# A hand-ordered linear-attention and FFN kernel: a neighbouring order of its 1639 steps

## The chip, the cores and the metric

The kernel runs on one core of a Trainium2 chip. The metric is device time in microseconds (us) of one execution, the median of several runs. Engines: TensorE (PE; its weight loads are shown apart as PEld), VectorE (DVE), ScalarE (ACT), GpSimd (POOL) and SyncE (SP), which only issues DMAs here. Each engine runs its own instructions strictly in the order in which the program lists them.

## The reference

```python
# q, k, v, alpha: (4, 8, 768, 48)
for t in range(S):                                    # 768 steps, a 48x48 state per head
    state = alpha[:, :, t, :, None] * state + einsum('bhd,bhe->bhde', k[:, :, t], v[:, :, t])
    y[:, :, t] = einsum('bhd,bhde->bhe', q[:, :, t], state)
x = y.transpose(0, 2, 1, 3).reshape(3072, 384)
h = x @ w_in                                          # w_in 384 x 2048
g = where(h > 0, h, exp(min(h, 0)) - 1)
out = g @ w_out                                       # w_out 2048 x 384
```

A gated linear attention with a decay per channel feeds a feed-forward network (FFN) with an ELU between its two products.

## The kernel before, in words

Time is cut into 24 windows of 128 steps (6 for each of 4 batches; eight heads as four pairs). The FFN works on 9 blocks of tokens: three narrow ones of 256, six wide ones of 384, and on 8 (narrow: pairs of) or 16 slices `j` of the hidden dimension. FFN products are split into a high and a low fp32r part, three matmuls for one product.

The program is a list of tokens, `ORDER`, written out by hand: `NAME.i` is one step for window, slice or block `i`, and a second number is a half, a part or a slice. The tokens are issued in exactly this order. Other tables give the PSUM bank (`BANKS`) and the SBUF slot (`SLOTS`) of each tile in order of use, and which engine takes a step: windows in `KAV`, `KBV`, `SQV` and slices in `WLV` run `KA`, `KB`, `SQ` and `WL` on DVE, the others on POOL; pairs in `GQ` have `GL` on POOL, the others on DVE.

The steps that matter here, by window `i`:

- Loads, all issued by SP: `LA` (alpha), `LB` (k for half 0, q for half 1), `L` (all of a window), `LV` (v), `F` (a slice of weights, as int64 words).
- DVE `SC` (L299): running product P of alpha. ACT `LN` (L311), `EX` (L317): R = 1/P. `KA` (L325), `KB` (L330), DVE `KC` (L335): the scaled keys; `KC` reads R. `SQ` (L353, L356): scaled queries. ACT `PC` (L340): a check sum of P, written over R.
- PE `TP` (L378): transposes the keys, ACT `KN` (L408) copies them out of PSUM; for later windows DVE `T` (L388) does it.
- PE `U` (L490, L472): two state products u[0] and u[1] of a window. For windows 0 and 1 they lie in one PSUM bank, in different columns; for later ones in two banks, which they share with the scores of `S`.
- `UA` reads u[0] (L507 on ACT for windows 0, 1, 6, 12, 18; L509 on DVE else); DVE `UB`, `UC` (L509, L538, L540) read u[1] and write the state for the next window. PE `UP` (L516) adds the state.
- PE `S` (L443, L427): scores, DVE `MK` (L460, L455) masks them out of PSUM. PE `YL` (L551), ACT `Y3` (L593), PE `Y` (L605, L551, L556): the output of a window; ACT `XH` (L619, L620), PE `XP` (L624) and `XL` (L642, L646): its high and low part, the input of the FFN.
- Weights: ACT `KW` (L686), DVE `DA` (L702), `DB` (L707) decode a slice, ACT `WH` (L734) and `WL` (L754) split it.
- FFN for block b, slice j: PE `A.b.j` (L786) is the first product, ACT `RA` (L795), `RB` (L800), DVE `RC` (L806) the ELU, ACT `GH` (L812) and `GL` (L819) split it, PE `O.b.j` (L835) is the second product. `Z` (L845) writes a block out.
- PE `X` (L208): filler matmuls with no result, in the first 12 us only.

Lines that a sentence can't say as well:

```python
def bank(name):
    return psa.tile([128, 512], F32, name=name, tag=f"pa{next(banks)}")
...
u = bank("u")[:, 0:2 * NP * D].rearrange("p (x n e) -> p x n e", x=2, n=NP)
d["u"] = [u[:, 0], u[:, 1]]
...
def PC(i):
    nc.scalar.activation(out=win[i]["R"], in_=pw(i), func=AF.Copy, accum_out=chk_p[:, 1, i:i + 1])
```

Of the kernel before, what the change touches and what calls it, by code (L numbers as in the profile page):

```python
# [63 lines left out]
WH.4 WL.4 KW.1.0 DA.1.0 RB.0.0 RC.0.0 DB.1.0 SC.5 RA.0.1 GH.0.0 UB.3 GL.0.0 L.4 RB.0.1 Y3.3 F.8 WH.1 A.0.3 RA.0.3 WL.1
WH.3 WL.3 XP.2 XL.2 F.10 RB.0.3 RC.0.1 Y.3 XH.3 LV.7 RC.0.3 UC.3 XL.3 KW.3 A.0.2 DA.3 SC.4 LN.5 A.1.1 DB.3 RA.0.2 RB.0.2
RA.1.1 EX.5 KA.5 O.0.0 RB.1.1 A.1.0 KW.4 RC.0.2 RC.1.1 RA.1.0 RB.1.0 GH.0.1 GL.0.1 GH.0.2 LN.4 F.12 DA.4 DB.4 WH.10
RC.1.0 GH.1.0 LC.1 A.1.3 KB.5 GL.1.0 WH.7 WH.8 WL.7 GH.1.1 F.9 GL.0.2 GL.1.1 A.1.2 O.0.1 RA.1.2 RB.1.2 WL.10 EX.4 O.1.0
CA.1 RC.1.2 KA.4 WH.5 WL.8 O.1.1 GH.1.2 WL.5 RA.1.3 RB.1.3 GL.1.2 A.1.5 RC.1.3 GH.0.3 F.14 ZV.6 KW.6 DA.6 CB.1 F.11
A.0.4 O.1.2 RA.0.4 RB.0.4 A.0.5 RA.1.5 O.0.2 KB.4 DB.6 WH.14 GL.0.3 SQ.4 KC.4 S.4 WH.12 RB.1.5 RA.0.5 RC.0.4 L.6 KC.5
RC.1.5 DA.5 GH.0.4 KW.5 LV.6 MK.4 TP.4 RB.0.5 GH.1.5 RC.0.5 KN.4 TP.5 KN.5 LC.3 DB.5 GH.1.3 O.0.3 PC.4 SQ.5 CA.3 LV.5  # L70
U.5 WH.9 WL.12 S.5 MK.5.1 MK.5.0 A.0.6 WH.11 WL.11 RA.0.6 GL.1.3 O.1.3 LV.4 U.4 RB.0.6 RC.0.6 PC.5 CB.3 SC.6 WL.9 LN.6
EX.6 GL.0.4 A.1.4 RA.1.4 RB.1.4 UA.4 UB.4 UC.4 L.7 SC.7 LN.7 KA.6 LC.2 RC.1.4 WL.14 A.1.6 KB.6 A.1.7 UA.5 GH.0.5 O.0.4
EX.7 KA.7 KB.7 RA.1.7 KC.6 RA.1.6 RB.1.7 RC.1.7 F.13 GH.1.4 GH.0.6 Y.5 RB.1.6 KC.7 T.7.2 GL.1.5 XH.5 Y.4 PC.7 RC.1.6
# [78 lines left out]
47251074320475130677466246740246271537464206
"""
# [942 lines left out]
```

## Time and profile before

| | us |
|---|---|
| median of 3 runs | 463.92 |
| lowest and highest run | 463.62, 464.58 |
| the profiled execution's own time | 463.38 |
| its span, first to last instruction | 461.6 |
| PE busy | 454.2 |
| DVE, ACT, POOL busy | 349.8, 327.7, 214.2 |

The span is 1.78 us shorter than that execution's time, and that execution is 0.54 us below the median of the runs. The rows further down are of this execution. A row of a timeline begins with its start and its length; brackets give the idle time of the engine before it and what ended that.

### The profile page before, as it was taken

To read this page: it belongs to the slowest core of one execution; us is meant where nothing else is said; L and a number is where in the kernel's file an instruction comes from. 1 tells how busy PE (TensorE), PEld (TensorE's weight loads), DVE (VectorE), ACT (ScalarE), POOL (GpSimd) and SP (SyncE) were. 2 spreads that over 40 slices of the span, in tenths; PEclk is the share of its full clock that TensorE was granted. 3 is DMA by queue.
4 is the path that set the end of the run, shared out by engine and by line. 5 is a ranking of instruction groups with operands and counts; after the bars stand their busy time and mean duration, and the time that the engine had idled before them with its cause. 6 is when DMAs were issued, how large, how long until landed. Compare 5 with 4: busy or idle time off the path is not lost.

```text
span 461.6 us, 12451 instructions
## 1 busy us (share of the span) xinstructions
PE 454.2 (98%) x4942; PEld 439.5 (95%) x4942; DVE 349.8 (76%) x756; ACT 327.7 (71%) x741; POOL 214.2 (46%) x185
## 2 busy tenths in 40 slices
...
GB/s 249 416 411 318 286 104 158 156 154 104 104 233 0 189 102 175 133 47 134 46 177 139 126 58 189 153 73 155 78 121 35 121 45 53 28 42 85 36 4 58
DMA packets 23859, 61.10 MB, mean 132 GB/s; under 512 B 3184, under 2 KB 10864, under 8 KB 23792
## 3 DMA queue, kind: packets, MB, share of 16 engines
...
q8 instruction: 41, 0.67, 0.6%
...
## 4 chain that ended last, share of the span: by engine, by line
PE 89%; DVE 4%; ACT 3%; DMA 3%; issue 1%; SPq 0%; DVEq 0%
PE h L786 39%; PE o L835 38%; PE y L556 4%; PE q L472 2%; PE q L427 2%; DMA vs<-in_vv_dram 2%; PE y L551 1%; ACT w L734 1%; DVE raw L702 1%; DVE wm L707 1%; DMA qka<-in_qka_dram 1%; ACT gh L812 1%; PE y L605 1%; ACT r L800 1%; PE sc L443 0%
## 5 line engine op out<-in xcount | busy, mean ns | idle before, releaser
L786 PE MATMUL h<-xt,w 128*128 128x384 f32 (+1 forms) x1296 | 200.0, 310 | 0.3 <-DVE r L806 0.3
L786 PEld LDWEIGHTS h<-xt,w 128*128 128x128 f32 x1296 | 190.7, 190 | 1.5 <-DVE r L806 0.4
L835 PE MATMUL o<-w,gh 128*128 128x384 f32 x768 | 188.3, 327 | 0.0
L819 POOL TENSOR_TENSOR gl<-r,gh 128x384 fp32r<-128x384 f32 (+1 forms) x90 | 106.4, 1189 | 158.1 <-ACT gh L812 101.8
L835 PEld LDWEIGHTS o<-w,gh 128*128 128x128 f32 x768 | 134.1, 189 | 0.5
L835 PE MATMUL o<-w,gl 128*128 128x384 f32 x384 | 125.3, 326 | 0.0
L795 ACT ACTIVATE r<-h 128x384 f32<-128x384 f32 (+1 forms) x120 | 60.3, 509 | 55.2 <-PE h L786 49.1
L388 DVE STREAM_TRANSPOSE kn<-qka 32x128 f32<-32x128 f32 x256 | 77.4, 303 | 4.2
L806 DVE SCALAR_TENSOR_TENSOR r<-r,h 128x384 f32<-128x384 f32 (+1 forms) x90 | 51.1, 577 | 37.9 <-ACT r L800 31.9
L835 PEld LDWEIGHTS o<-w,gl 128*128 128x128 f32 x384 | 72.6, 189 | 0.2 <-POOL gl L819 0.2
L800 ACT ACTIVATE r<-r 128x384 f32<-128x384 f32 (+1 forms) x120 | 64.0, 543 | 2.0
L812 ACT CAST gh<-r 128x384 fp32r<-128x384 f32 (+1 forms) x90 | 46.4, 529 | 18.6 <-DVE r L806 16.1
L356 POOL TENSOR_TENSOR st<-qka,P 64x512 f32<-64x512 f32 x34 | 43.0, 1263 | 17.4 <-DVE P L299 16.1
L455 DVE TENSOR_TENSOR st<-q,mask 64x256 f32<-64x256 f32 x76 | 32.1, 422 | 9.2 <-PE q L427 6.0
L325 POOL TENSOR_TENSOR qka<-qka,R 128x512 f32<-128x512 f32 x16 | 21.0, 1313 | 29.9 <-ACT R L317 24.7
L806 DVE SCALAR_TENSOR_TENSOR h<-r,h 128x384 f32<-128x384 f32 (+1 forms) x30 | 17.4, 588 | 20.7 <-ACT r L800 20.3
L299 DVE TENSOR_TENSOR_SCAN P<-qka,first 128x516 f32<-128x516 f32 (+1 forms) x25 | 30.7, 1233 | 0.5 <-DMA qka<-in_qka_dram 0.3
L819 DVE TENSOR_TENSOR gl<-h,gh 128x384 fp32r<-128x384 f32 (+1 forms) x30 | 17.3, 582 | 17.9 <-ACT gh L812 7.5
L725 ACT ACTIVATE ck<-ck,lim 128x384 f32<-128x384 int32 x32 | 25.4, 793 | 0.6
L720 ACT ACTIVATE ck<-ck,lim 128x384 int32<-128x384 int8 x32 | 25.4, 793 | 0.0
L311 ACT ACTIVATE R<-P 128x512 f32<-128x512 f32 (+1 forms) x25 | 15.4, 615 | 11.3 <-DVE P L299 11.2
L812 ACT CAST gh<-h 128x384 fp32r<-128x384 f32 (+1 forms) x30 | 14.8, 495 | 8.9 <-DVE h L806 8.0
...
## 6 DMA issues: line engine op xcount, KB each, us to landing
...
```

The costliest lines, as they stand in the source:

```text
L299: nc.vector.tensor_tensor_scan(out=P[:, n].rearrange("p n w -> p (n w)"), data0=t[:, 2 * NP * W + n.start * AW:2 * NP * W + n.stop * AW], ...
L356: eng(SQV, i).tensor_tensor(out=st[r, a], in0=d["q"][r], in1=pw(i)[r], op=ALU.mult)
L388: nc.vector.transpose(out=kn[32 * t:32 * t + 32, :, 32 * g:32 * g + 32], in_=d["kt"][32 * g:32 * g + 32, :, 32 * t:32 * t + 32])
L455: nc.vector.tensor_tensor(out=d["st"][r, a, :, c * C:(c + 1) * C], in0=d["s4"][a][o], in1=mask[o].unsqueeze(1).broadcast_to([64, NP, C]), ...
L720: nc.scalar.activation(out=ck[f][:, :, 0], in_=t, func=AF.Abs, scale=9.0 / 64, bias=lim[:, 0:1])
L786: nc.tensor.matmul(h[:, y, :], lhsT=t[:, wi, ws], rhs=x[:, c, xi].rearrange("p (a x) -> p x a", a=2), start=(y == 0 and k == 0), stop=(k = ...
L795: nc.scalar.activation(out=r, in_=d["h"], func=AF.Relu, scale=-1.0)
L800: nc.scalar.activation(out=d["r"], in_=d["r"], func=AF.Exp, scale=-1.0)
L806: nc.vector.scalar_tensor_tensor(out=d["g"], in0=d["r"], scalar=-1.0, in1=d["h"], op0=ALU.add, op1=ALU.max)
L812: nc.scalar.copy(out=gh, in_=d["g"])
L819: q.tensor_tensor(out=gl, in0=d["g"], in1=d["gh"].bitcast(F32), op=ALU.subtract)
L835: nc.tensor.matmul(o[:, 0:DM], lhsT=gt[:, y, ms], rhs=t[:, wi, f * DM:f * DM + DM].rearrange("p (a x) -> p x a", a=2), start=(u == 0 and y ...
```

## The change

No function changes. The same 1639 tokens stand in a neighbouring order, and the tables follow: `BANKS` and `SLOTS` are new throughout, `WL.4` goes from POOL to DVE, `KA`, `KB` and `SQ` of a few windows change engine, 14 `GL` go from POOL to DVE and 18 from DVE to POOL. On PE the order of products changes in many places; early, `A.0.1` comes right behind `A.0.0`, and the attention steps `U.3 Y.2 YL.3` stand together behind both.

Around windows 0 and 1, as listed before and after (tokens of SP, PE, ACT and DVE mixed):

```diff
-LA.0.0 SC.0.0 LN.0.0 EX.0.0 LA.0.1 SC.0.1 LB.0.0 LN.0.1 KA.0.0 LV.0.0 KB.0.0 EX.0.1 KC.0.0 TP.0.0 KA.0.1 KB.0.1 KC.0.1
-PC.0 X.4.1 TP.0.1 KN.0 LA.1 SC.1 LB.1.1 LB.0.1 LN.1 X.3.2 U.0 SQ.1 SQ.0 EX.1 S.0 LB.1.0 KA.1 KB.1 KC.1 X.2.0 UC.0 L.2
-SC.2 UA.0 TP.1 KN.1 LV.1.0 MK.0 LN.2 EX.2 S.1 MK.1 SQ.2 U.1 PC.1 LV.0.1 F.0 YL.0 Y3.0 KW.0.0 DA.0.0 KA.2 KB.2 F.2 UP.1
-KC.2 UC.1 KW.0.1 PC.2 UA.1 Y.0 XH.0 TP.2 DA.0.1 DB.0.1 L.3 SC.3 KN.2 LN.3 SQ.3 DB.0.0 S.2 LV.2 U.2 UA.2 LV.1.1 YL.1 Y3.1
-EX.3 XP.0 Y.1 WH.2 XL.0 WH.0 F.6 MK.2 YL.2 KA.3 KB.3 KC.3 TP.3 WL.0 XH.1 KN.3 XP.1 XL.1 S.3 WL.2 F.4 KW.2 F.3 DA.2 Y3.2
...
+LA.0.0 SC.0.0 LA.0.1 SC.0.1 LN.0.0 EX.0.0 LB.0.0 KA.0.0 LB.0.1 LN.0.1 EX.0.1 KB.0.0 KC.0.0 TP.0.0 KA.0.1 KB.0.1 KC.0.1
+LA.1 X.4.1 SC.1 LB.1.1 SQ.1 TP.0.1 KN.0 LV.0.0 U.0 LB.1.0 LN.1 EX.1 SQ.0 X.3.2 KA.1 S.0 L.2 LV.1.0 LV.0.1 PC.0 X.2.0
+KB.1 KC.1 TP.1 PC.1 KN.1 UA.0 UC.0 S.1 SC.2 MK.0 LN.2 EX.2 F.0 U.1 MK.1 UP.1 UA.1 KA.2 YL.0 UC.1 F.2 Y3.0 Y.0 KB.2
+KW.0.1 DA.0.0 KC.2 PC.2 XH.0 TP.2 KW.0.0 KN.2 SQ.2 S.2 DA.0.1 L.3 DB.0.1 LV.1.1 SC.3 LN.3 LV.2 XP.0 XL.0 YL.1 Y3.1
+EX.3 U.2 DB.0.0 WH.0 F.6 F.4 MK.2 WH.2 UA.2 Y.1 KA.3 XH.1 KB.3 KC.3 YL.2 TP.3 LV.3 XP.1 PC.3 WL.2 KN.3 XL.1 F.3 KW.2
...
```

The other parts of the diff that the text below speaks of:

```diff
-WLV, KAV, KBV, SQV = (0, 2, 7, 8, 10, 11, 13, 15),  \
-    (0, 1, 2, 3, 6, 7, 14, 22),  \
-    (0, 1, 2, 3, 4, 7, 11, 22, 23),  \
-    (0, 1, 18, 19)
+WLV, KAV, KBV, SQV = (0, 2, 4, 7, 8, 10, 11, 13, 15),  \
+    (0, 1, 2, 3, 7, 13, 15, 20),  \
+    (0, 1, 2, 3, 4, 6, 7, 18),  \
+    (0, 1, 21)
...
```

Every line of `ORDER` differs. On PE alone, the first FFN products run `A.0.0 Y.2 U.3 A.0.1 YL.3 A.0.3` before and `A.0.0 A.0.1 U.3 Y.2 YL.3 A.0.3` after; around slice 9 of block 3 they run `A.3.9 O.3.6 A.3.10 A.3.12 A.4.3 O.3.7 O.3.8 A.3.15 O.3.9` before and `A.3.15 A.3.9 O.3.8 A.4.3 O.3.9` after, with `GL.3.9` moved to DVE; around `A.1.4` they run `A.0.6 O.1.3 U.4 A.1.4` before and `A.0.6 U.4 O.1.3 A.1.4` after.

## Rows read from the trace of the kernel before

**Rows 1.** The page: busy us, share of the span and instructions by engine.
```profile
PE 454.2 (98%) x4942; PEld 439.5 (95%) x4942; DVE 349.8 (76%) x756; ACT 327.7 (71%) x741; POOL 214.2 (46%) x185
```
**Rows 2.** Stretches of the span: busy us (instructions) of PE, PEld, DVE, ACT, POOL; granted clock.
```profile
0.00:26.70 26.70, 23.98 (x421) 17.18 (x421) 23.73 (x46) 17.06 (x41) 5.77 (x15) 1.00 0.93 343
26.70:77.20 50.50, 50.21 (x606) 48.64 (x602) 46.98 (x54) 47.74 (x80) 31.78 (x18) 1.00 0.67 242
...
457.20:461.60 4.40, 0.00 (x1) 0.00 (x0) 0.00 (x0) 0.48 (x1) 0.00 (x0) 1.00 0.27 98
```
**Rows 3.** Waits of PE: us in total, times, longest.
```profile
PE h L786 <- DVE r L806: 0.3, 1, 0.3
```
**Rows 4.** The chain that ended last, 180 to 200 us: start, us, what.
```profile
190.17 1.66 PE h L786 x9
...
194.76 1.46 PE h L786 x9
```
**Rows 5.** Timeline of PE in the head.
```profile
11.14 0.61 PE L208 MATMUL xf<-wz 128*128 128x512 bf16 x2
12.33 0.66 PE L378 MATMUL tp<-ident,qka 128*128 128x128 f32 x4 [0.58 <-DVE qka L335]
...
20.53 0.68 PE L472 MATMUL q<-vs,kn 64*64 64x48 f32 x32 [0.49 <-DMA vs<-in_vv_dram]
...
24.90 0.63 PE L378 MATMUL tp<-ident,qka 128*128 128x128 f32 x4
...
26.71 2.27 PE L786 MATMUL h<-xt,w 128*128 128x256 f32 x18
```
**Rows 6.** Timeline of ACT in the head.
```profile
8.20 0.56 ACT L408 COPY kn<-tp 128x512 f32<-128x512 f32 x1
8.71 0.63 ACT L311 ACTIVATE R<-P 128x512 f32<-128x512 f32 x1
...
12.64 0.33 ACT L507 ACTIVATE vs<-u 128x192 f32<-128x192 f32 x1 [2.54 <-DVE vs L540]
13.03 0.58 ACT L408 COPY kn<-tp 128x512 f32<-128x512 f32 x1
```
**Rows 7.** Timeline of DVE in the head.
```profile
11.59 0.69 DVE L335 SCALAR_TENSOR_TENSOR qka<-R,qka 128x512 f32<-128x512 f32 x1
12.20 0.35 DVE L540 SCALAR_TENSOR_TENSOR vs<-u,P 128x192 f32<-128x192 f32 x1
...
18.51 0.96 DVE L707 SCALAR_TENSOR_TENSOR wm<-raw 128x768 int32<-128x768 int32 x1 [0.22 <-ACT raw L686]
...
22.65 0.69 DVE L325 TENSOR_TENSOR qka<-qka,R 128x512 f32<-128x512 f32 x1 [0.25 <-ACT R L317]
...
24.11 0.69 DVE L335 SCALAR_TENSOR_TENSOR qka<-R,qka 128x512 f32<-128x512 f32 x1
```
**Rows 8.** Timeline of ACT around UA.18.
```profile
282.65 0.66 ACT L507 ACTIVATE vs<-q 48x192 f32<-48x192 f32 x2 [1.56 <-DVE st L455]
```
**Rows 9.** Timeline of DVE there: the two halves of MK.18.1.
```profile
282.19 0.88 DVE L455 TENSOR_TENSOR st<-q,mask 64x256 f32<-64x256 f32 x2
```
**Rows 10.** Groups by line and shape: count, busy us, mean ns, idle us before.
```profile
L388 DVE STREAM_TRANSPOSE kn<-qka 32x128 f32<-32x128 f32 x256 | 77.4, 303 | 4.2
...
L800 ACT ACTIVATE r<-r 128x384 f32<-128x384 f32 x96 | 48.9, 521 | 1.7
L795 ACT ACTIVATE r<-h 128x384 f32<-128x384 f32 x96 | 46.0, 486 | 51.7 <-PE h L786 45.8 <-POOL gl L819 3.4 <-PE o L835 2.1
...
L806 DVE SCALAR_TENSOR_TENSOR r<-r,h 128x384 f32<-128x384 f32 x72 | 38.7, 551 | 37.2 <-ACT r L800 31.6 <-issue 4.9
L812 ACT CAST gh<-r 128x384 fp32r<-128x384 f32 x72 | 35.5, 507 | 15.1 <-DVE r L806 13.7 <-PE o L835 0.7 <-ACT gh L812 0.4
...
L819 DVE TENSOR_TENSOR gl<-h,gh 128x384 fp32r<-128x384 f32 x24 | 13.2, 555 | 17.0 <-ACT gh L812 6.5 <-POOL gl L819 5.6 <-PE o L835 4.8
...
L754 DVE TENSOR_TENSOR w<-wm,w 128x768 fp32r<-128x768 f32 x5 | 4.9, 999 | 0.1
```

More of the change, by code (lines that the diff above doesn't have):

```diff
@@ L64 @@
[L64 to L73, printed above, removed]
@@ new lines @@
+KW.5 RC.0.4 SQ.4 S.4 RA.0.5 RB.0.5 KC.5 PC.5 TP.5 RC.1.5 SQ.5 KN.5 DA.5 RC.0.5 TP.4 MK.4 DB.5 KN.4 O.0.3 LV.5 S.5 LC.3
+MK.5.1 U.5 WL.12 A.0.6 GH.0.4 GL.0.4 CA.3 WH.9 CB.3 WH.11 RA.0.6 RB.0.6 LV.4 MK.5.0 PC.4 WH.14 L.7 WL.11 U.4 UA.4
+RC.0.6 UB.4 GL.1.3 SC.6 UC.4 O.1.3 GH.1.5 A.1.4 A.1.6 UA.5 LN.6 WL.9 RA.1.4 GH.0.6 SC.7 EX.6 LC.2 RB.1.4 LN.7 RA.1.6
+EX.7 WL.14 A.1.7 RB.1.6 RA.1.7 RB.1.7 RC.1.4 KA.6 O.0.4 KB.6 KA.7 KC.6 KB.7 RC.1.7 Y.5 CA.2 KC.7 T.7.2 GH.1.4 PC.6
+GL.1.5 GH.0.5 XH.5 Y.4 GL.1.4 XH.4 RC.1.6 XL.5 GH.1.6 F.15 F.13 DA.7 XL.4 TP.6 O.1.4 O.1.5 SQ.6 KN.6 KW.7 CB.2 DB.7
@@ new lines @@
+LC.9 A.4.0 RC.4.3 CA.9 CB.9 SQ.14 GH.3.13 RA.4.0 A.4.4 KC.14 T.14.1 A.4.1 O.3.12 L.16 RA.4.1 RB.4.1 LC.6 GL.3.13
+O.3.13 RA.4.4 T.14.0 GH.3.15 RB.4.4 T.14.2 MK.13.1 RC.4.1 MK.13.0 RC.4.4 GL.3.15 T.14.3 CA.6 CB.6 O.3.14 O.3.15 UC.13
+GH.4.1 GL.4.1 U.14 LC.8 RB.4.0 RC.4.0 GH.4.0 GL.4.0 Z.3.0 S.14 UA.14 Y.13 UB.14 XH.13 SC.15 SQ.15 MK.14.1 Y.12 MK.14.0
+LN.15 XH.12 EX.15 A.4.8 RA.4.8 LV.15 RB.4.8 XL.13 XD.13 PC.14 XL.12 Z.3.1 A.4.13 RA.4.13 A.4.2 RA.4.2 RB.4.2 O.4.0
+RB.4.13 UC.14 KA.15 SC.16 A.4.7 Z.3.2 RC.4.2 KB.15 CA.8 KC.15 T.15.1 RC.4.8 T.15.0 CB.8 RA.4.7 T.15.2 RB.4.7 RC.4.7
@@ new lines @@
+T.15.3 A.4.12 RA.4.12 A.4.5 RB.4.12 O.4.1 GH.4.2 RA.4.5 A.4.6 LN.16 GL.4.2 GH.4.3 RB.4.5 GL.4.3 O.4.2 O.4.3 RC.4.5
+RC.4.13 EX.16 KA.16 SQ.16 RC.4.12 U.15 LC.10 CA.10 PC.15 S.15 UA.15 XD.12 GH.4.4 UB.15 UC.15 RA.4.6 GH.4.7 GL.4.4
+RB.4.6 GL.4.7 Y.14 GH.4.5 RC.4.6 GL.4.5 CB.10 MK.15.0 GH.4.6 A.4.9 O.4.4 GL.4.6 L.17 SC.17 O.4.5 XH.14 A.4.11 XL.14
+MK.15.1 RA.4.9 GH.4.8 RB.4.9 RC.4.9 GH.4.9 KB.16 KC.16 T.16.0 T.16.1 PC.16 A.4.10 T.16.2 LN.17 EX.17 KA.17 GL.4.8
+RA.4.10 KB.17 XD.14 ZV.18 T.16.3 LC.11 CA.11 A.4.15 RA.4.15 O.4.6 LV.17 O.4.7 GL.4.9 RB.4.15 A.4.14 RA.4.14 KC.17
@@ new lines @@
+LN.21 O.5.12 GL.5.14 O.5.13 LV.20 LC.19 O.5.14 O.5.15 Z.5.0 Z.5.1 A.6.9 RA.6.9 GH.6.0 S.20 U.20 UA.20 UB.20 UC.20
+MK.20.0 EX.21 CA.19 Y.19 XH.19 MK.20.1 KA.21 LV.23 GL.6.0 Z.5.2 RB.6.9 CB.19 RC.6.9 A.6.3 KB.21 A.6.5 RA.6.5 RB.6.5
+RA.6.3 RB.6.3 SC.22 A.6.4 RC.6.1 RA.6.4 KC.21 T.21.3 A.6.8 A.6.10 GH.6.1 PC.21 LV.21 RB.6.4 RC.6.4 O.6.0 SQ.21 RA.6.10
+RB.6.10 RC.6.3 GL.6.1 O.6.1 RC.6.10 LC.21 GH.6.2 GL.6.2 A.6.7 A.6.6 GH.6.3 GL.6.3 RC.6.5 RA.6.8 RB.6.8 RC.6.8 O.6.2
+T.21.2 CA.21 CB.21 XL.19 T.21.0 GH.6.4 O.6.3 RA.6.7 GL.6.4 O.6.4 GH.6.5 RB.6.7 GL.6.5 RC.6.7 GH.6.8 RA.6.6 GH.6.7
```

153 lines of the change are left out of this document (72 added, 81 removed), and 8 rows, old and new, of the table GQ.

## The prediction

> **What bounds the kernel now.** I read the busy shares first. PE is busy for 454.2 of 461.6 us [rows 1], so an order can give back only what PE loses outside its products. Next the stretches, to see where it loses: 2.72 us up to 26.7 us, 0.29 us up to 77.2 us, nothing from there to 457.2 us, and 4.40 us in the tail, where the last block is copied and written out [rows 2]. The granted clock is 1.00 in all of them, the upper level of 2.4 GHz. The waits of PE name the 0.29: one first product (`A.1.4`, at 77.15 us) waited 0.3 for DVE [rows 3]. So from `A.0.0`, which starts at 26.71 us [rows 5], to the end, PE works without a break that could be closed. The chain of waits shows what is left there: a wide `A` takes 1.46 us behind an FFN product and 1.66 behind an attention step [rows 4], so each island of attention steps inside the FFN stream costs some 0.20.
>
> In the head the order of things is different. In the first 26.7 us DVE is busy for 23.73 us [rows 2], and `SC`, `KA`, `KB`, `KC` of four windows run behind each other on it; `TP.3` starts at 24.90, right when `KC.3` ends (24.11 + 0.69), and `XP.1`, `S.3`, `A.0.0` follow it without a gap [rows 5, 7]. So DVE sets when `A.0.0` starts, and a microsecond that DVE loses before `KC.3` is a microsecond for the whole kernel: behind `A.0.0` there are 430.5 us of PE work that nothing shortens.
>
> **The change part by part.**
>
> *UA.0 and UC.0.* This is the part that I hold to decide. `UA.0` (ACT) reads u[0] and `UC.0` (DVE) reads u[1] of window 0, two column ranges of one bank. Before, `UC.0` is listed first: it runs on DVE at 12.20, right behind `KC.1` [rows 7], and `UA.0` waits on ACT until it has ended, 2.54 us, named by its releaser `vs L540`, which is `UC.0` [rows 6]. Neither reads what the other writes, so what orders them is the bank. The same is seen at 282.65: `UA.18` on ACT waits for DVE `L455`, the masks [rows 8], and begins after the first half of `MK.18.1` (282.19 + 0.44), which reads the bank of u[0], not after its second half, which reads another bank [rows 9]. In each case the step listed later waits.
>
> The new list has `KC.1 TP.1 PC.1 KN.1 UA.0 UC.0`. Now `UC.0` waits for `UA.0`, and `UA.0` stands on ACT behind `PC.1`, which overwrites the R that `KC.1` reads, and behind `KN.1`, which needs `TP.1`, which needs `KC.1`. `KC.1` still ends at 12.28 (11.59 + 0.69) [rows 7]. `PC.1` then fills ACT up to about 13.0, and `KN.1` starts as before at 13.03 [rows 6]. The step behind a `KN` started 0.51 us after it (8.20 to 8.71) [rows 6], so `UA.0` starts at 13.54 and ends at 13.87 (0.33 long); with 0.05 for the hand-over `UC.0` starts at 13.92. That is 1.72 us later than 12.20. On DVE `SC.2`, `MK.0`, `MK.1` and all else stand behind `UC.0`, so DVE has nothing to run from 12.28 to 13.92.
>
> The Trainium skill (PSUM — Partial Sum Buffer, section on PSUM bank collisions) says that reads by ScalarE and VectorE of one bank in the same partitions collide too, whatever the columns, so that software must order them. The trace agrees with it in the 2.54 us; by that rule the sum is the one below, and by a rule that went by address `UC.0` would stay at 12.20 (the first rival).
>
> *From UC.0 to KC.3.* Before, DVE goes from `UC.0` to `KC.3` in 11.91 us (12.20 to 24.11), with two waits in it, 0.22 and 0.25 [rows 7]. The new list has the same steps there. If both waits vanish, `KC.3` is 1.72 - 0.47 = 1.25 late, the lower bound. But `DA.0.0`, which stood between `MK.1` and `KA.2`, now comes behind `KB.2`, so `KA.2` has to wait for `EX.2`; the 0.25 that `KA.3` waits for `EX.3` [rows 7] is the nearest row. Besides, `UA.1` is now listed ahead of `UC.1`, and `Y3.0` stands on ACT behind `UA.1`, which waits for `UP.1`. With 0.25 more and none of the old waits gone it is 1.97; with 0.25 twice, 2.22, the upper bound. I take 1.9, since the 0.22 depends on `KW.0`, which has more time now.
>
> *Moves that cost nothing.* `LB.0.1` is loaded earlier and `LV.0.0` later, behind `LA.1` and `LB.1.1` on SP's queue; `U.0` needs it, and `X.3.2` now follows `U.0` and delays `S.0`. What hides this is the time until `TP.1`: from 11.14 to 12.33 PE has only fillers (0.61) and a wait for `KC.1` [rows 5]. Without that cover each 0.1 would count. The other way round, `U.2` waited 0.49 for `LV.2` [rows 5]; it is listed behind `YL.1` now and everything is later, so that wait goes, but `KC.3` and not `U.2` is what `TP.3` waited for, so nothing is gained: late next is `KC.3`. `Y.0` loses the cover of `UP.1` for `Y3.0`; `TP.2` behind it waits longer for `KC.2`.
>
> *Behind A.0.0.* The step from `KC.3` to `A.0.0` stays at 2.60 us (24.11 to 26.71): `TP.3`, `XP.1`, `S.3` in the same order. `A.0.1` right behind `A.0.0` joins two islands to one, 26 to 25 in all, counted on the two lists: -0.2. `WL.4` comes to DVE (1.0) and `GL.1.0` leaves it (0.555 for 384 columns, so 0.74 for its 512) [rows 10]: 0.26 more on DVE before `RC.0.6`, the step for which `A.1.4` waited. The new list gives `A.1.4` a bank of `U.4`, which is free after `UA.4`, one `RC` (0.551 for 384 columns, so 0.73 here) earlier on DVE. I take 0 for the two together: -0.3 if the wait goes, +0.3 if DVE's work shows.
>
> *Second products close behind their first.* The tightest is `O.3.9`, with two FFN groups between, 2 x 1.46 = 2.92 us, and 0.33 more until the `gl` part is wanted. The steps between sum to 0.486 + 0.521 + 0.551 + 0.507 + 0.555 = 2.62 [rows 10], so a margin of 0.63 is left for five hand-overs and for queueing. Bounded by nothing below, and by one `T.13.3` in front of `RC.3.9` (four transposes of 0.303, 1.2) above. Of the 32 moved `GL` none has as little; where POOL or DVE has a queue, some tenths may come. I take 0.2 for all, with 0 and 1.5 as ends.
>
> **The sum.** Against the profiled execution's own 463.38: +1.9 (head) - 0.2 (island) + 0 + 0.2 = +1.9, which is 465.3. The median of the runs is 0.54 above that execution, so 465.8 is the forecast for the median. Its own range: +1.25 - 0.2 - 0.3 = +0.75, 464.7, up to +2.2 - 0.2 + 0.3 + 1.5 = +3.8, 467.7.
>
> **The rivals.**
>
> 1. *Same: DVE is not held.* If reads of different columns need no order, `UC.0` stays at 12.20. What is left of the head is `Y3.0` behind `YL.0` and `UA.1` (some 0.5 us on ACT and PE), and the island: -0.2 to +0.5, 463.7 to 464.4. Against it speak the two waits [rows 6, 8]. The same time comes out if DVE makes good the loss in later waits; against that, DVE is busy for 46.98 of the 50.50 us that follow [rows 2]. Chance 0.14.
> 2. *Faster: PE's waits close.* If `UC.0` is not held and the loads fall better, the 0.49 before `U.2`, the 0.29 at `A.1.4` and 0.2 for the island go: -1.0, 462.9. It decides once `KC.3` ends before 24.8. Nothing in the trace lets `UA.0` on ACT start before `KC.1` ends. Chance 0.07.
> 3. *Slower still: the clock falls.* PE gets waits in the head that it did not have, some 0.4 to 0.7 us each before `YL.0`, `Y.0`, `TP.2` and `U.2`. So far the granted clock held at 1.00 with waits of 0.58 and 0.49 [rows 2, 5]. At 1.2 GHz a stretch of 3 us of products would take 3 us more: 468.8. The Trainium skill (TensorE: Matmul & The Clock Gate, section on the HAM clock gate) says that an idle array falls to the lower clock; no row here shows it after the start. Chance 0.06.
>
> The forecast itself has 0.73.
>
> **How the numbers follow.** About 0.2% (0.93 us) is what a measurement of this kernel can tell from no change, so slower means above 464.85. Slower gets the forecast's 0.73 less 0.03 for its lowest end, and the clock's 0.06: 0.76. Same gets 0.14 and that 0.03: 0.17. Faster keeps 0.07. For the range I leave out the faster rival, most of the same one and the clock: 464.2 to 467.7.
>
> **What would show it.** In the changed kernel's timeline of DVE a gap of about 1.6 us before `UC.0` (L540), ended by ACT L507; `UC.0` near 13.9; `KC.3` near 26.0; `A.0.0` on PE near 28.6; from there to PE's end 430.3 us. A wait of PE before some `O` (L835) would show the last term. The prediction is wrong if `UC.0` does not wait, if DVE reaches `KC.3` less than 1 us late, or if PE, once in the FFN, shows gaps of more than 1.5 us in all.

## The result and the profile after

The changed kernel takes 468.13 us (median of 20 runs, 467.25 to 468.99) and the kernel before 463.95 us in the same rounds: a ratio of 1.0084, 95% interval 1.0073 to 1.0095. It is slower by 4.2 us. The forecast was 465.8 with a range up to 467.7: the sign is right, the size is a little under half of what came.

The profiled execution took 468.99 us, with a span of 467.3, 5.6 us more than that of before; that is 0.9 us above the median, and its tail is 0.9 us longer than that of before. The page's busy shares, against [rows 1]:

```profile
PE 455.7 (98%) x4942; PEld 440.4 (94%) x4942; DVE 350.0 (75%) x750; ACT 327.7 (70%) x741; POOL 215.2 (46%) x191
```

PE's work has grown by 1.5 us, and of that 1.17 is the longer start (busy until `A.0.0` begins, fillers and waits between small products counted as busy). The shares alone name no engine for the rest. The stretches up to `A.0.0`, to 104 us, to PE's end and the tail (the columns of [rows 2]):

```profile
0.00:29.10 29.10, 25.15 (x422) 17.58 (x422) 24.13 (x46) 17.55 (x43) 5.76 (x15) 1.00 0.95 361
29.10:104.00 74.90, 72.85 (x903) 70.84 (x900) 70.80 (x87) 63.35 (x114) 45.59 (x27) 1.00 0.57 198
104.00:462.00 358.00, 357.73 (x3624) 351.93 (x3622) 255.09 (x619) 246.32 (x585) 163.85 (x149) 1.00 0.33 99
462.00:467.30 5.30, 0.00 (x0) 0.00 (x0) 0.00 (x0) 0.48 (x1) 0.00 (x0) 0.94 0.23 83
```

`A.0.0` starts at 29.10, which is 2.39 later than in [rows 5]. Of this, 0.36 is there from the first step, since `KA.0.0` begins that much later. The start of `KA.0.0` differs between profiled executions (4.80 to 5.58 with the changed order of the first loads, 4.73 to 5.18 with that of before), so the 0.36 is not shown to come from the list. Then PE is idle for 74.90 - 72.85 = 2.05 us up to 104 us, where before it had lost 0.29 [rows 2]; behind 104 us it is idle for 0.27. The granted clock is 1.00 wherever PE works. So there are two losses, one ahead of `A.0.0` and one between 29 and 104 us. Line numbers are one higher than before. The waits of PE, against [rows 3], show where the second one lies (total, times, longest):

```profile
PE y L606 <- ACT y L594: 1.3, 2, 0.7
PE q L428 <- DVE xt L647: 1.2, 1, 1.2
PE q L473 <- PE h L787: 0.7, 1, 0.7
PE h L787 <- DVE r L807: 0.2, 1, 0.2
```

The first line is the head (`Y.0`, `Y.1`). L428 is `S.6`, which waits for `XL.4` on DVE, and L473 is `U.4`, which overwrites the banks that DVE reads in `MK.5.1` and `MK.5.0`. Its row names PE; that it waits for DVE is read from the times, since its two pieces begin 0.08 and 0.14 us behind the last reads of the two banks.

What they cost is read from the starts of steps that stand in both lists. At `S.4` PE is 2.02 us late (69.01 against 66.99). From `A.0.6` to `A.1.4` it takes 6.11 us against 5.13, which is 0.98 for `U.4`; from `S.6` to `O.0.5` it takes 2.06 against 0.60, which is 1.46 for `S.6`. Together this is 2.44, and PE is 4.38 us late at `O.0.5` and 4.76 at its last product.

The head, in the timelines of DVE, ACT and PE. On DVE, against [rows 7], `KC.1`, `UC.0` and `KC.3`:

```profile
11.95 0.69 DVE L336 SCALAR_TENSOR_TENSOR qka<-R,qka 128x512 f32<-128x512 f32 x1
14.24 0.36 DVE L541 SCALAR_TENSOR_TENSOR vs<-u,P 128x192 f32<-128x192 f32 x1 [1.60 <-ACT vs L508]
...
25.99 0.69 DVE L336 SCALAR_TENSOR_TENSOR qka<-R,qka 128x512 f32<-128x512 f32 x1
```

On ACT, against [rows 6], `PC.1`, `KN.1` and `UA.0`:

```profile
12.67 0.63 ACT L341 ACTIVATE R<-P 128x512 f32<-128x512 f32 x1 [1.59 <-DVE qka L336]
...
13.39 0.58 ACT L409 COPY kn<-tp 128x512 f32<-128x512 f32 x1
13.87 0.34 ACT L508 ACTIVATE vs<-u 128x192 f32<-128x192 f32 x1
```

And on PE, against [rows 5], `Y.0`, `Y.1`, `TP.3` and `A.0.0`:

```profile
17.77 0.87 PE L606 MATMUL y<-y,sel 64*64 64x128 f32 x12 [0.66 <-ACT y L594]
...
23.94 0.87 PE L606 MATMUL y<-y,sel 64*64 64x128 f32 x12 [0.64 <-ACT y L594]
...
25.98 0.71 PE L552 MATMUL y<-st,vs 64*48 64x64 f32 x18 [0.33 <-issue]
...
27.26 0.66 PE L379 MATMUL tp<-ident,qka 128*128 128x128 f32 x4
29.10 1.16 PE L787 MATMUL h<-xt,w 128*128 128x256 f32 x8
```

DVE stands for 1.60 us in front of `UC.0`, ended by `UA.0` on ACT (L508), and `KC.3` comes 1.88 us later than before; 1.52 of that is the list's own, counted from `KA.0.0`. What the prediction had not seen is that PE itself is late: `Y.1` waits 0.64 for `Y3.1` (L594), which stands on ACT behind `LN.3` and `XL.0`, and then stands for 0.33 in its own products with nothing in the profile that it waits for (`issue`). `TP.3` starts at 27.26, although `KC.3` has ended at 26.68.

The second loss is read best from the chain of waits. In it PE's own work is the whole chain from 26 to 63 us. Then the chain passes over to DVE and stays off PE until `S.6` (start, us, what):

```profile
80.58 2.73 DVE P L300
83.31 0.02 issue
83.33 0.63 ACT R L312
...
85.58 0.07 issue
85.65 1.40 POOL qka L326
...
88.45 0.07 DVE qka L336
88.52 1.54 issue
...
97.03 0.55 DVE xt L647
97.58 0.14 issue
97.71 0.69 PE q L428 x30
```

Two things in it are long for no reason that the list gives: `SC.6` (L300) at 2.73, and 1.54 "issue" inside `KC.6` (L336). The timeline of DVE with the same two, and that of POOL:

```profile
80.49 2.81 DVE L300 TENSOR_TENSOR_SCAN P<-qka,first 128x516 f32<-128x516 f32 x1
...
84.73 1.23 DVE L300 TENSOR_TENSOR_SCAN P<-qka,first 128x516 f32<-128x516 f32 x1
...
88.37 1.76 DVE L336 SCALAR_TENSOR_TENSOR qka<-R,qka 128x512 f32<-128x512 f32 x1
```

```profile
80.38 1.83 POOL L755 TENSOR_TENSOR w<-wm,w 128x768 fp32r<-128x768 f32 x1 [1.87 <-ACT w L735]
...
88.29 1.29 POOL L820 TENSOR_TENSOR gl<-r,gh 128x512 fp32r<-128x512 f32 x1 [1.25 <-PE o L836]
```

`SC.7`, the same instruction, takes 1.23; `SC.6` takes 2.81, and `WL.14` on POOL began 0.11 us ahead of it. `KC.6` takes 1.76 instead of 0.69, and `GL.1.5` on POOL began 0.08 ahead of it. In the trace of before `SC.6` began 0.46 us ahead of `WL.14`; there `SC.6` took 1.59 and `WL.14` 2.77, and `KC.6` was through before `GL.1.5` began.

### The profile page after: what moved, and what is told of

It reads as the page before. It is cut to its first block, busy times and chain, and to the rows that moved or that the text cites. A ratio compares the mean times of both kernels' runs of the same rounds, so it can differ in the third digit from the quotient of the medians.

```text
span 467.3 us, 12472 instructions
## 1 busy us (share of the span) xinstructions
PE 455.7 (98%) x4942; PEld 440.4 (94%) x4942; DVE 350.0 (75%) x750; ACT 327.7 (70%) x741; POOL 215.2 (46%) x191
## 4 chain that ended last, share of the span: by engine, by line
PE 87%; DVE 6%; ACT 2%; issue 2%; DMA 1%; POOL 1%; ACTq 0%; DVEq 0%; POOLq 0%
PE h L787 38%; PE o L836 36%; PE y L557 3%; PE q L428 2%; PE q L473 2%; PE wp L209 1%; DVE raw L703 1%; PE y L552 1%; DMA out_dram<-ot 1%; DVE P L300 1%; DVE r L807 1%; DVE qka L336 1%; PE sc L444 1%; PE tp L379 1%; PE u L491 1%
## 5 line engine op out<-in xcount | busy, mean ns | idle before, releaser
L820 POOL TENSOR_TENSOR gl<-r,gh 128x384 fp32r<-128x384 f32 (+1 forms) x94 | 103.4, 1106 | 146.8 <-ACT gh L813 77.2
L807 DVE SCALAR_TENSOR_TENSOR r<-r,h 128x384 f32<-128x384 f32 (+1 forms) x94 | 53.2, 577 | 39.3 <-ACT r L801 36.6
L813 ACT CAST gh<-r 128x384 fp32r<-128x384 f32 (+1 forms) x94 | 49.1, 531 | 31.1 <-DVE r L807 19.1
L801 ACT ACTIVATE r<-r 128x384 f32<-128x384 f32 (+1 forms) x120 | 65.2, 547 | 2.5
L357 POOL TENSOR_TENSOR st<-qka,P 64x512 f32<-64x512 f32 x36 | 46.6, 1294 | 10.4 <-DVE P L300 6.6
L300 DVE TENSOR_TENSOR_SCAN P<-qka,first 128x516 f32<-128x516 f32 (+1 forms) x25 | 33.7, 1350 | 0.6 <-DMA qka<-in_qka_dram 0.3
L807 DVE SCALAR_TENSOR_TENSOR h<-r,h 128x384 f32<-128x384 f32 (+1 forms) x26 | 15.2, 590 | 18.0 <-ACT r L801 17.6
L820 DVE TENSOR_TENSOR gl<-h,gh 128x384 fp32r<-128x384 f32 (+1 forms) x26 | 14.9, 578 | 15.1 <-ACT gh L813 9.6
L331 POOL TENSOR_TENSOR R<-P,R 128x512 f32<-128x512 f32 x16 | 21.4, 1335 | 8.1 <-DVE qka L326 7.6
```

Source lines behind the costliest of these rows:

```text
L300: nc.vector.tensor_tensor_scan(out=P[:, n].rearrange("p n w -> p (n w)"), data0=t[:, 2 * NP * W + n.start * AW:2 * NP * W + n.stop * AW], ...
L357: eng(SQV, i).tensor_tensor(out=st[r, a], in0=d["q"][r], in1=pw(i)[r], op=ALU.mult)
L801: nc.scalar.activation(out=d["r"], in_=d["r"], func=AF.Exp, scale=-1.0)
L807: nc.vector.scalar_tensor_tensor(out=d["g"], in0=d["r"], scalar=-1.0, in1=d["h"], op0=ALU.add, op1=ALU.max)
L813: nc.scalar.copy(out=gh, in_=d["g"])
L820: q.tensor_tensor(out=gl, in0=d["g"], in1=d["gh"].bitcast(F32), op=ALU.subtract)
```

## The experiments

Each kernel was timed in five rounds beside the kernel before (463.4 to 463.9 us in these rounds). The ratio is to that.

**Three waits, one by one.** The first theory after the result was that the changed list has three separate waits (`UC.0`, `U.4`, `S.6`), each of which can be taken back by moving one step.

```diff
-KC.1 TP.1 PC.1 KN.1 UA.0 UC.0                      (e1_uc_first)
+KC.1 UC.0 TP.1 PC.1 KN.1 UA.0
-WL.11 U.4 UA.4 RC.0.6 UB.4 GL.1.3 SC.6 UC.4 O.1.3  (e2_u4_late)
+WL.11 GL.1.3 O.1.3 U.4 UA.4 RC.0.6 UB.4 SC.6 UC.4
-XL.5 GH.1.6 F.15 F.13 DA.7 XL.4 TP.6               (e3_xl4_early)
+XL.5 XL.4 GH.1.6 F.15 F.13 DA.7 TP.6
```

> The changed kernel with UC.0 listed right behind KC.1 again, ahead of UA.0; nothing else. Theory (separate waits: the hold of UC.0 in the head, U.4 listed ahead of O.1.3, XL.4 listed behind DA.7): the DVE gap of 1.60 us before UC.0 goes, A.0.0 starts about 1.7 us earlier (27.4 instead of 29.1), the waits of PE at U.4 and S.6 stay, 466.4 us. Rival (one cause: DVE is late from the head on, and U.4 and S.6 only show it again): all three go, 463.9 to 464.5 us. Second rival (the bank does not matter, something else holds UC.0): 468.1 us.

> The changed kernel with O.1.3 and GL.1.3 listed ahead of U.4, as before; nothing else. Separate waits: the two waits of PE at U.4 (0.68 and 0.22 by the waits, some 1.1 us of lost time against before) are covered by the 2.05 us of O.1.3, 467.1 us. One cause: the next step that needs DVE, A.1.4 or A.1.6, waits instead, 467.8 to 468.2 us.

> The changed kernel with XL.4 listed right behind XL.5, ahead of DA.7 (1.9 us on DVE); nothing else. S.6 takes the PSUM bank that XL.4 reads. Separate waits: the wait of PE in S.6 (1.15 us by the waits, 1.5 us of lost time) goes, 466.6 us. One cause: DVE is as late as it was and the next consumer of its work waits, 467.8 to 468.2 us.

> The changed kernel with the three edits together. Separate waits add up: 468.1 - 1.7 - 1.1 - 1.5 = 463.8 us, level with the kernel before. If they overlap: 464.5 to 466 us.

Measured: e1_uc_first 466.71 (1.0063, 1.0049 to 1.0077), e2_u4_late 467.77 (1.0085, 1.0072 to 1.0099), e3_xl4_early 468.38 (1.0096, 1.0079 to 1.0113), e4_all_three 466.25 (1.0062, 1.0048 to 1.0076). Only the first may give something back: it is 3.3 us behind the kernel before in the same rounds, where the changed kernel was 4.2 behind, and the two intervals just touch. In e2_u4_late the waits of PE stand before and behind `U.4` instead (0.5 and 0.75); in e3_xl4_early `S.6` no longer waits, and `A.2.1` waits, for the step of DVE (`UC.6`) that frees its bank:

```profile
102.87 2.25 PE L787 MATMUL h<-xt,w 128*128 128x256 f32 x18 [1.32 <-DVE vs L539]
```

So the theory of separate waits fell for `U.4` and `S.6`. Whoever comes next in PE's order and needs DVE pays; DVE is late, and not those steps.

**The head alone, and the bank.** In e6_before_head the list of before has one thing of the change: `UA.0` listed ahead of `UC.0`.

```diff
-X.2.0 UC.0 L.2 SC.2 UA.0 TP.1 KN.1
+X.2.0 L.2 TP.1 KN.1 UA.0 UC.0 SC.2
```

> The order of before, with UA.0 ahead of UC.0 as in the changed kernel and nothing else: UC.0 and SC.2 stand behind UA.0. The step of the prediction (UC.0 held by UA.0's read of the same bank, KC.3 and with it A.0.0 later by up to 1.9 us, nothing given back) says 464.8 to 465.6. If later slack takes it up: 463.5 to 464.0. If it grows on the way: over 466.

In e15_two_banks the changed list stays, and u[1] of window 0 gets a bank of its own.

```diff
         d["u"] = [u[:, 0], u[:, 1]]
+        if i == 0:
+            d["u"][1] = bank("u")[:, 0:2 * NP * D].rearrange("p (x n e) -> p x n e", x=2, n=NP)[:, 1]
...
-BANKS 7012345671...
+BANKS 70121345671...
```

> The changed kernel, its list untouched, with the two products of window 0 that UA.0 and UC.0 read put into two PSUM banks (the second one takes the bank of the warm-up X.4.1). The prediction's cause, that UC.0 is held because it reads the bank that ScalarE reads: the 1.60 us of idle time on VectorE goes, UC.0 starts at about 12.4 and the kernel is as fast as e1_uc_first, 466.4 to 467.0. Rival that the list's place holds it (an engine takes its work in that order whatever the bank): 467.8 to 468.5.

Measured: e6_before_head 465.17 (1.0035, 1.0023 to 1.0047), so the one exchange costs 1.8 us. In its trace `A.0.0` is 2.15 us late; 0.36 of that comes back at `A.1.4`, whose wait in [rows 3] closes, and 1.75 is left at the last product. e15_two_banks takes 466.42 (1.0058, 1.0040 to 1.0076): it is 2.8 us behind the kernel before in the same rounds, against 4.2 for the changed kernel, and the intervals just touch. `UC.0` in their timelines of DVE, first e6_before_head, then e15_two_banks:

```profile
13.86 0.36 DVE L539 SCALAR_TENSOR_TENSOR vs<-u,P 128x192 f32<-128x192 f32 x1 [1.60 <-ACT vs L506]
```

```profile
12.21 0.35 DVE L543 SCALAR_TENSOR_TENSOR vs<-u,P 128x192 f32<-128x192 f32 x1
```

The same wait to the hundredth, ahead of `UC.0`, made in a list that did not have it; and gone, with the list untouched, once the two reads are of different banks. It is the bank. In e15_two_banks `KC.3` begins at 24.69, which is 0.58 later than before: what is left of the loss up to there when the bank no longer orders the two reads.

**Where the rest is lost.** e13_join_banks runs the list and the division of work of before up to `A.2.1` (about 104 us, where both lists have issued nearly the same steps) and the changed ones behind it. A first form of it, e11_join, took its banks behind the joint by a rule of its own.

> The order and division of work of before up to A.2.1 (about 104 us), where both lists have issued nearly the same steps, and those of the changed kernel behind it, with the O steps close behind one another; PSUM banks and rings behind the joint are given to whichever has been free longest. Theory that all of the loss lies ahead of 104 us: 463.0 to 464.2. Rival that the later order (tight second products, its end) costs something: 464.5 to 466.

> The joint of e11_join at the same place, but with the changed kernel's own PSUM banks and ring buffers behind it (renumbered once, so that what lives across the joint keeps its place), since e11_join waited 3.8 us in O.2.0 for a bank that the renumbering by longest free had given it. Theory that all of the loss lies ahead of 104 us: 463.3 to 464.4. Rival that the later order costs something: 465 to 467.

Measured: e13_join_banks 463.84 (1.0000, 0.9983 to 1.0017). All that the change does behind 104 us, the second products close behind the first included, costs or brings no more than its interval leaves open, 0.17% (0.8 us) either way. Behind the start (1.1) PE's longest waits in it are 0.5 in the head (`TP`) and 0.4 (total, times, longest):

```profile
PE h L787 <- DVE r L807: 0.7, 2, 0.4
PE tp L379 <- DVE qka L336: 0.5, 1, 0.5
```

e11_join took 469.0 (1.0101, 1.0080 to 1.0122); PE stood for 3.8 us in `O.2.0`, in a bank that the rule had given it right behind `TP.9`, for which `KN.9` had still to come. That is a loss by its banks and says nothing of the order.

**The division of work.** e5_before_split puts the changed division of the early steps on the list of before; e7_uc_and_split does the reverse on e1_uc_first.

```diff
-WLV (0, 2, 7, ...)      KAV (..., 6, ...)  KBV (...)     GQ (... 1.3 ...)
+WLV (0, 2, 4, 7, ...)   KAV (...)          KBV (... 6)   GQ (... 1.0 1.3 ...)
```

> The order of before, with the changed kernel's division of work for the early steps alone: WL.4 from GpSimd to VectorE, KA.6 from VectorE to GpSimd and KB.6 the other way, GL.1.0 from VectorE to GpSimd. Theory that VectorE sets TensorE's pace up to about 104 us: the net VectorE work added (WL.4 +0.97, GL.1.0 -0.70, KA.6 and KB.6 a wash, and some stretching of VectorE instructions that run beside a GpSimd one) comes out at the end, 464.2 to 465.2 against 463.5. Rival that only the head's order matters: 463.5 to 463.9.

> The changed kernel with UC.0 ahead of TP.1 (as in e1_uc_first, 466.7) and with the early division of work of before (WL.4 and KB.6 on GpSimd, KA.6 and GL.1.0 on VectorE). If VectorE's load between 30 and 100 us is what e1_uc_first still lost: 464.3 to 465.5. If the order of the steps alone loses it: 466.4 to 467.

Measured: e5_before_split 469.5 (1.0128, 1.0106 to 1.0149) and e7_uc_and_split 471.63 (1.0173, 1.0159 to 1.0187). Both are far slower than either expectation; both divisions are worse on the other's list. In e5_before_split `WL.4` on DVE (0.96) is absorbed: the steps around it are as early as before. The loss has two parts. The first is holds on DVE: `GL.1.0`, now on POOL, runs beside `WL.7`, and `WL.10`, late by that, begins just behind `KA.4` on POOL, which is where it was. The timeline of DVE at `WL.7`, `GL.0.2` with `GL.1.1`, and `WL.10`, and that of POOL below:

```profile
51.93 2.00 DVE L754 TENSOR_TENSOR w<-wm,w 128x768 fp32r<-128x768 f32 x1 [1.76 <-ACT w L734]
53.86 1.27 DVE L819 TENSOR_TENSOR gl<-h,gh 128x512 fp32r<-128x512 f32 x2
55.06 2.02 DVE L754 TENSOR_TENSOR w<-spare,w 128x768 fp32r<-128x768 f32 x1
```

```profile
51.83 1.28 POOL L819 TENSOR_TENSOR gl<-r,gh 128x512 fp32r<-128x512 f32 x1
54.97 1.29 POOL L325 TENSOR_TENSOR qka<-qka,R 128x512 f32<-128x512 f32 x1 [1.85 <-DMA vs<-in_vv_dram]
```

`WL.7` and `WL.10` took 0.96 and 0.95 in the trace of before. Each is now 1.05 longer, since an instruction of POOL began 0.1 us ahead of it. DVE's lateness steps up by 1.05 and 1.07 there and by 1.13 at `SC.7`, beside `KA.6`, which this edit gives to POOL. The second and larger part is PE's wait for a weight (total, times, longest):

```profile
PE h L786 <- POOL w L754: 2.5, 1, 2.5
```

This is `WL.14`, read in `A.1.7`. It stands on POOL behind `KA.6`, which waits 2.59 there for `EX.6`, so `WL.14` begins at 82.83 instead of 77.47. PE is 1.5 us late at `A.1.4`, 5.9 at `O.0.5`, and the kernel is 6.1 us slower.

**Taking the two held instructions out of POOL's way.** e8_no_overlap puts `WL.14` and `GL.1.5` on DVE. e9_sc6_later only moves `SC.6` behind `UC.4` and `UA.5`, which read PSUM; e10_uc_sc6 adds e1's edit.

```diff
-UB.4 GL.1.3 SC.6 UC.4 O.1.3 GH.1.5 A.1.4 A.1.6 UA.5 LN.6 WL.9 RA.1.4 GH.0.6 SC.7 EX.6 LC.2 RB.1.4
+UB.4 GL.1.3 UC.4 O.1.3 GH.1.5 A.1.4 A.1.6 UA.5 SC.6 LN.6 WL.9 RA.1.4 GH.0.6 SC.7 EX.6 LC.2 RB.1.4  (e9)
+UB.4 GL.1.3 UC.4 O.1.3 GH.1.5 A.1.4 A.1.6 UA.5 SC.6 WL.9 RA.1.4 RB.1.4 LN.6 GH.0.6 SC.7 EX.6 LC.2  (e12)
```

> The changed kernel with the two GpSimd instructions that run beside SC.6 and KC.6 (WL.14, GL.1.5) put on VectorE instead. If a VectorE instruction is stretched by the GpSimd one beside it: SC.6 takes 1.2 to 1.6 us instead of 2.81 and KC.6 0.7 instead of 1.76, VectorE has 1.0 + 0.7 more of work and 2.3 to 2.7 less of stretching, 467.1 to 467.9 at the end. If their length has another cause: both stay long and the kernel loses the added work, 469 to 470.

> The changed kernel with SC.6 moved behind UC.4 and UA.5 on VectorE, so that WL.14 on GpSimd no longer starts just ahead of it; no engine does more or less work. Theory that what is lost behind the head is VectorE's instructions with two SBUF inputs held by a GpSimd one that started first: SC.6 falls from 2.81 to 1.2 to 1.6 us and the kernel from 468.1 to 466.8 to 467.2. Rival that the loss lies in the waits of U.4 and S.6 or in the sum of VectorE's work: no change, 467.7 to 468.5.

> e9_sc6_later with UC.0 ahead of TP.1 as in e1_uc_first (466.7) too. If both losses are separate and both on the way that sets the end: 465.2 to 465.8. If SC.6's comes back at the next GpSimd instruction: 466.5 to 466.9.

Measured: e8_no_overlap 469.77 (1.0130, 1.0115 to 1.0146), e9_sc6_later 467.9 (1.0080, 1.0062 to 1.0099), e10_uc_sc6 466.56 (1.0056, 1.0039 to 1.0073). The mechanism shows: `SC.6` falls from 2.81 to 1.22 and 1.23, and in e8_no_overlap `KC.6` from 1.76 to 0.68. The time does not follow. In e8_no_overlap `WL.14` on DVE comes so late that PE waits 1.7 us for it inside `A.1.7`, and `WL.14` is itself held to 1.97. In e9_sc6_later DVE has saved 1.57 and then stands, for the `RB.1.4` of ACT (L800):

```profile
82.46 2.36 DVE L299 TENSOR_TENSOR_SCAN P<-qka,first 128x516 f32<-128x516 f32 x2
86.52 0.69 DVE L806 SCALAR_TENSOR_TENSOR r<-r,h 128x512 f32<-128x512 f32 x1 [1.71 <-ACT r L800]
```

ACT runs in the order of the list, and `LN.6`, which needs `SC.6`, stands ahead of `RA.1.4` and `RB.1.4` there; and `SC.6` ends at 83.69, no earlier than before its move (83.30). So e12_sc6_ln6 moves `LN.6` too, and e14_uc_u4_sc6 adds the edits of e1 and e2.

> The changed kernel with SC.6 behind UC.4 and UA.5 as in e9_sc6_later, and LN.6 behind RB.1.4 on ScalarE as well, since in e9_sc6_later RA.1.4 still stood behind LN.6, which needs SC.6. Theory that VectorE's lateness at SC.6 goes by way of ScalarE's order to RC.1.4 and from there, without a gap, to XL.4 and UC.6: RC.1.4 starts 1 to 2 us earlier, KC.6 may start before GL.1.5 and take 0.7, the wait of S.6 (1.56) goes, 466.3 to 467.0. If it stays at 467.7 or above, what sets S.6 and A.2.1 is still something else.

> e12_sc6_ln6 with UC.0 ahead of TP.1 and with U.4 behind O.1.3 too: 464.2 to 465.4 if the head's hold, the wait of U.4 and VectorE's stretch at SC.6 are what the changed kernel loses; 466 or more if one of them only hides another.

Measured: e12_sc6_ln6 467.2 (1.0070, 1.0043 to 1.0097), e14_uc_u4_sc6 465.9 (1.0044, 1.0027 to 1.0061). In e12_sc6_ln6 (`RC.1.4`, `KB.6`, then `KC.6` and `KB.7`):

```profile
84.10 0.69 DVE L806 SCALAR_TENSOR_TENSOR r<-r,h 128x512 f32<-128x512 f32 x1
86.25 0.69 DVE L330 TENSOR_TENSOR R<-P,R 128x512 f32<-128x512 f32 x1 [1.46 <-POOL qka L325]
...
87.46 0.69 DVE L335 SCALAR_TENSOR_TENSOR qka<-R,qka 128x512 f32<-128x512 f32 x1
88.06 1.77 DVE L330 TENSOR_TENSOR R<-P,R 128x512 f32<-128x512 f32 x1
```

`RC.1.4` comes 2.0 us earlier than in the changed kernel and `KC.6` is no longer held. But `KB.6` now waits 1.46 for the later `EX.6` and `KA.6`, and the hold by `GL.1.5` falls on `KB.7`. At `UC.6` DVE is 0.71 earlier than in the changed kernel, and 0.43 of that it had brought along from `MK.5.1`. The interval of e12_sc6_ln6 overlaps that of the changed kernel, and that of e14_uc_u4_sc6 those of e1 and e4, so no gain by freeing single instructions is shown. In these runs a hold that is taken from one instruction comes down on another. A last order, e12_uc_sc6_gl15, was e10_uc_sc6 with `GL.1.5` listed behind `GL.1.4`, to free `KC.6`; 464.3 to 465.3 us was expected, but in that order steps wait for each other in a circle, and it has no time.

**Taking most of GpSimd's reads away.** So that a hold can't move on, every `GL` of blocks 0 and 1 and every `WL` that is on POOL becomes a fill of its output with zeros: in the kernel before, in the changed one, and in e1_uc_first. These kernels leave out the low parts of those products, so they show times and are no kernels to use. `KA`, `KB` and `SQ` stay on POOL and read as they did.

```diff
+        if b < 2 and inr(b, j):                                  # in GL
+            nc.gpsimd.memset(gl.bitcast(F32), 0.0)
+            return
...
+            if f not in WLV:                                     # in WL
+                nc.gpsimd.memset(wgts[f][:, 1].bitcast(F32), 0.0)
+                return
```

> The kernel before, with every GpSimd GL of blocks 0 and 1 and every GpSimd WL replaced by a fill of its output with zeros, which reads nothing (so those low parts are left out of the products). VectorE is then not held by them. Since TensorE works without a break from 26.7 us there, at most its one wait before A.1.4 (0.6) goes: 462.9 to 463.7 by either theory.

> The changed kernel with the same fills in place of those GpSimd instructions (their low parts are left out). Theory that the second loss is VectorE held by GpSimd instructions that read SBUF: most of it goes and the head's loss is left, 465.0 to 466.2. Rival that VectorE's order and amount of work lose it, whatever GpSimd does: 467.3 to 468.2.

> e16_after_fill with UC.0 ahead of TP.1 as in e1_uc_first: by the theory both losses are gone, 463.3 to 464.6, about level with e17_before_fill; by the rival 465.8 to 466.8.

Measured: e17_before_fill 463.77 (1.0005, 0.9997 to 1.0014), e16_after_fill 465.41 (1.0040, 1.0023 to 1.0057), e18_uc_fill 464.1 (1.0003, 0.9994 to 1.0012). Each lies where the theory put it or within 0.1 of that: the fills give the kernel before nothing, the changed one 2.4 us (1.8 behind the kernel before in the same rounds instead of 4.2), and with `UC.0` ahead as well the two lists are level. In e16_after_fill `SC.6` and `KC.6` take their own time, and PE is idle for 0.07 us from 28 to 104 us (the columns of [rows 2]), against 2.05:

```profile
79.47 1.23 DVE L300 TENSOR_TENSOR_SCAN P<-qka,first 128x516 f32<-128x516 f32 x1
...
86.58 0.68 DVE L336 SCALAR_TENSOR_TENSOR qka<-R,qka 128x512 f32<-128x512 f32 x1
```

```profile
28.00:104.00 76.00, 75.93 (x949) 73.73 (x950) 68.93 (x92) 68.57 (x126) 23.54 (x28) 1.00 0.61 214
```

Some holds are left in it: `WL.10`, `WL.7` and `WL.8`, beside `KB.5`, `KA.4` and `SQ.4` on POOL, still take 1.88, 1.92 and 1.92, and PE loses nothing by them. The gain lies later: from 61 us to `MK.5.1` DVE catches up 2.46 us against the changed kernel, without a wait in either, because its instructions are shorter.

A fill also is shorter (0.5 for `GL`, against 1.29) and does not wait for ACT's `GH` or `WH`, and these three runs alone do not exclude that this helps. Against it speaks that PE's two waits in the changed kernel were for DVE, and not for a `gl` or a `w`, and that a fill which begins first does not lengthen the instruction beside it, as `KC.4` in e16_after_fill shows (1.08 in the changed kernel):

```profile
67.69 0.76 POOL L756 MEMSET w<- 128x768 f32 x1 [3.63 <-issue]
...
68.08 0.69 DVE L336 SCALAR_TENSOR_TENSOR qka<-R,qka 128x512 f32<-128x512 f32 x1
```

No run beats the kernel before. e13_join_banks is level with it with all the work done; of the changed lists with all the work done e14_uc_u4_sc6 is the fastest, 0.44% behind.

## Why the prediction was right, and where it failed

*`UA.0` and `UC.0`.* Right, in mechanism and size. The idle time was to be 1.6 us, ended by ACT L507, and is 1.60; `UC.0` was to be 1.72 late and is 2.04, of which 0.36 was there from the first step and 1.68 is the hold. e15_two_banks shows that the bank is the cause: the two reads are ordered by their bank, as forecast, and the first rival, that columns decide, fell.

*From `UC.0` to `KC.3`.* +1.9 was forecast and +1.88 measured, which is partly luck: 0.36 of it is the first step, and the list's own part is 1.52. From `UC.0` to `KC.3` DVE takes 11.75 us, 0.16 less than before, where some 0.2 more had been taken. The head alone, on the list of before, costs 1.8 us at the end (e6_before_head): as forecast, DVE does not make it good behind.

*"The step from KC.3 to A.0.0 stays at 2.60 us."* It is 3.11 in this execution, and 2.60 holds for the list. The wait of `Y.1` for `Y3.1`, which the prediction did not see, stands in the other runs with the changed head as well, and by itself it costs nothing. In e2_u4_late, where it is there and `Y.1` has no break in its own products, the step is 2.60 (`KC.3` on DVE, then `A.0.0` on PE):

```profile
25.95 0.69 DVE L335 SCALAR_TENSOR_TENSOR qka<-R,qka 128x512 f32<-128x512 f32 x1
```

```profile
28.55 0.71 PE L786 MATMUL h<-xt,w 128*128 128x256 f32 x4
```

The break costs the 0.5. It comes in some executions and not in others, with the same steps (0.33 in the changed kernel and 0.66 in e9_sc6_later, where the step is 3.45), and what causes it stays open.

*"I take 0 for the two together": the failing step.* Behind `A.0.0` the prediction allowed DVE's lateness 0.3 us either way, from one `WL` more, one `GL` less and one bank. Measured are 2.44 us more on PE, 0.98 at `U.4` and 1.46 at `S.6`. The reckoning had counted what DVE has to do, at durations from rows where nothing was in the way. But the durations depend on what POOL does at that moment. From `KC.3` to `SC.7` DVE takes 58.74 us against 55.99 before. Of the 2.75 more, some 1.8 is that instructions of the same kind take longer. Another 0.3 is `WL.4` for `GL.1.0`, which the prediction had right, and 0.7 is `UA.5`, which is listed ahead of `SC.7` now; waits are 0.4 shorter, and some 0.3 is spread over the rest. So DVE is 3.0 us late at `MK.5.1` and 4.6 at `SC.7`, where the head had left it 1.9 late. A row that was read warns of it: DVE busy for 46.98 of 50.50 us [rows 2]; the prediction drew from it that DVE would not make good a loss, and not that it would pass on each new one.

What is shown of this second loss: it lies ahead of 104 us (e13); it is not in the steps that wait, since moving them moves the wait (e2, e3); instructions of DVE are held while POOL works (e5, e8, e9); and without POOL's `GL` and `WL` it is gone (e16, e18), while the kernel before gains nothing from the same (e17), where PE's only wait between 26.7 us and the tail was 0.3 [rows 3]. Nor is it a follow-up of the first: with the head repaired (e1, e15), PE still takes 432.1 to 432.4 us from `A.0.0` to its last product, against 432.5 in the changed kernel, 430.2 before and 429.6 in e16. What is not settled is which of the holds counts for how much. Besides `SC.6` and `KC.6`, five instructions ahead of 75 us (`SC.4`, `WL.10`, `WL.7`, `KB.4`, `DB.5`) are each 0.4 to 0.6 longer than before and two (`WL.8`, `DA.6`) 0.5 and 0.3 shorter; e7, meant to take the division of work apart, made new holds of its own.

*Second products.* 0.2 was taken, 0 to 1.5 allowed; no `O` waits, `O.3.9` included, so the term is 0. There is one new wait of 0.2 at a first product, `A.7.6`, for a `RC` on DVE (L807 in the list of waits), and e13_join_banks has it too (0.4). *The clock* held at 1.00, so the third rival fell.

By terms, in the profiled execution: forecast +1.9 (head) + 0 - 0.2 + 0.2. Found at `A.0.0` is +2.39: 1.52 is the list's, 0.36 the first step and 0.51 the break in `Y.1`. Up to `S.4` 0.37 comes back, where 0.2 was forecast for the island. Then +0.98 (`U.4`), +1.46 (`S.6`) and 0.3 in small pieces make up the 4.76 at PE's last product.
